# The end of a fused FFT, MLP and soft-MoE kernel rebuilt: weights and constants loaded during the last batch from ScalarE's queue, sums transposed before they are divided, four output homes

## The chip, the cores and the metric

The kernel runs on one core of a Trainium2 chip. The metric is the device time of one launch in microseconds, as the median of several runs. Every number below is from one profiled execution of the kernel before, unless it is called a median. Engines are named as in the profile: PE (TensorE), PEld (its weight loads), DVE (VectorE), ACT (ScalarE), POOL (GpSimd), SP (SyncE, which here only issues DMAs).

## The reference, cut to what is computed

```python
X = fft(fft(x, axis=1), axis=2).real              # x: 8 x 3072 x 256
x = X.reshape(8 * 3072, 256)
h = x @ w_in                                      # 256 -> 2048
x = (h - tanh(h)) @ w_out                         # 2048 -> 256
logits = x @ phi                                  # 32 slots: 8 experts x 4
d = exp(logits - logits.max(0)); d /= d.sum(0) + 1e-9      # over all tokens
slot_input = (d.T @ x).reshape(8, 4, 256)
for e in range(8):
    slot_out[e] = relu(slot_input[e] @ w1[e]) @ w2[e]      # 256 -> 1024 -> 256
c = exp(logits - logits.max(1)); c /= c.sum(1) + 1e-9      # over the slots
return c @ slot_out.reshape(32, 256)              # 24576 x 256, 25.17 MB
```

## The kernel before, in words

The work has three stages. A short head brings the weights into shape. The main stage walks over eight batches in 384 steps of a tile each, about 3.1 us a step: a DFT of 24 rows on POOL and ACT, matrix DFTs and the wide product on PE (`wide`, L462), tanh on ACT (`act_h`, L489), a split of tanh in two 16-bit halves written to a ring of 16 places called `tr` (`act_t` on ACT, L497; `low_t` on DVE, L501), a DMA transpose of each place issued by SP (`turn_t`, L505, from `tr` to `tt`), logits on PE (`logits`, L532), and, every eight steps (a pair of tiles), a running softmax over the tokens whose weighted sums gather in `zacc` (128x130) and `acc` (128x512, `acc_add`, L644). The logits of each pair are parked in DRAM (`lsd`) for the second softmax.

The end, from about 1281 us on, is strictly sequential at first. (1) The last pair's softmax: `soft_e` (L595) is its first step on ACT, `acc_add` (L644) its last. (2) The sums are divided by the softmax's sum and turned: `total` (L1308), `norm` (L1311), `a_norm` and the scaling of `zacc`, then `a_turn` (L1320) and `z_norm_t` (L1325). (3) `slot_in` (L1342, L1345) multiplies them by `w_out` (`wot`) and by `WW`, and `slot_in_t` turns the slots. (4) The experts, four side by side in two groups `eg`: `up` (L1380) by `w1`, relu, a turn (`up_t`, L1386), `down` (L1392) by `w2`; `place` (L1399) and `placed` (L1403 to L1406) put the results into `R`. (5) For each batch the second softmax on the logits read back (`c_max` to `c_lo`), its turn on PE (`c_t`, L1487), the product with `R` (`mix`, L1514, 12 pairs of products a batch), the copy of each pair out of PSUM (`mixed`) into an output home `ot`, and the store (`store`, L1525; batch 0 in pairs, L1531).

The order on every engine is decided when the kernel is built, by a list scheduler (`Flow`). An operation is added with estimated costs by engine, with keys that it reads and writes, and with rings from which it takes a buffer; the scheduler then emits each engine's instructions in the order of its own estimate. `put` sorts the main stage's operations by a planned step. `late` makes an operation less urgent. On the chip every engine, and every queue that issues DMAs, works through its list in order.

Before, all DMAs are issued by SP. Twelve halves of `w1` (512 KB each, experts 0 to 5) go into rows of the two `x` buffers during the last batch. The other loads stand behind the last transposes in SP's list: the logits of four batches, `w_out`, `w1` of experts 6 and 7 and the constants (`late_consts`: `in_ct`, which holds the identity and the small matrices, and `wwd`, which holds `WW`), which take tiles that the main stage has given up, and then the 16 halves of `w2` (512 KB each) into places of `tr`. PSUM's eight banks are divided in the end: four for products, two for turns, two for the rest. Two output homes, `xbs[0]` and `xbs[1]`, take turns.

Of the kernel before, what the change touches and what calls it, by code (L numbers as in the profile page):

```python
# [21 lines left out]
D = 256  # L22
# [33 lines left out]
DLAG = 14.0  # L56
HLATE = 0.0
HEAD = 3
# [168 lines left out]
def fft_mlp_softmoe_kernel(ctx: ExitStack, tc: tile.TileContext, x, w_in, w_out, phi, w1, w2, cq, fd, cm, ct, out):  # L227
# [82 lines left out]
    tA = tmp.tile([128, 4, 256], F32, name="tA")  # L310
    tB = tmp.tile([128, 4, 256], F32, name="tB")
# [732 lines left out]
    wot, late_consts = [], []  # L1044

    def w1_part(e, k):
        ny.dma_start(out=w1s[e][:, k, :], in_=w1[e, 128 * k:128 * k + 128, :])
# [6 lines left out]

    def wo_unit(k):
# [4 lines left out]
    lt4 = []  # L1060

    def lt_unit(b):
        if not lt4:
            lt4.append(wbp.tile([128, 4, 24, NS], F32, tag="cqs", name="lt4"))
        ny.dma_start(out=lt4[0][:, b], in_=lsd_of(b))

    def wl_unit(e, k):
        if e == 6 and k == 0:
            w = wbp.tile([128, 2, 2, FE], F32, tag="Wl", name="wlw")
            w1s[6], w1s[7] = w[:, 0], w[:, 1]  # L1070
        w1_part(e, k)

    def w128_unit(k):
        if k == 0:
            late_consts.append(wbp.tile([128, 2048], F32, tag="W128", name="w128w"))
            ny.dma_start(out=late_consts[0][:, 0:608], in_=ct)
        else:
            ny.dma_start(out=late_consts[0][:, 608:1120], in_=wwd)
# [99 lines left out]
    stage(soft_e, NP, 8, {"A": 0.55}, lambda p: ([("LT", p), nb_(p), nb_(p, 1), ("dT", p), ("lk", p)], [("e", p)], "fac", f"B:LT{p} ls"))  # L1178
# [98 lines left out]
    main.close()  # L1277

# [12 lines left out]
    X = {}  # L1291
    fl.add({"D": DLAG}, lambda _: None, w=["behind"])


    rs = tl.tile([128, 1], F32, name="rs")
    zn = tl.tile([128, 130], F32, name="zn")
    wx = cts[:, 1120:2048]
    an, tn = wx[:, 0:512], tl.tile([128, 4, 4, NS], F32, name="tn")
    zz = tl.tile([128, 2, NS], F32, name="zz")
    si = tl.tile([128, 256], F32, name="si")  # L1300
    st = tl.tile([128, 256], F32, name="st")
# [3 lines left out]
    def total(_):  # L1305
        X["a"] = ps1.tile([128, 1], F32, tag="a", name="rsp")
        for r in range(0, 128, NS):
            nt.matmul(X["a"][r:r + NS], part[0], zacc[:, 0:1], start=True, stop=True, tile_position=(0, r))  # L1308
# [5 lines left out]
    def a_norm(_):  # L1314
        nv.tensor_scalar(out=an, in0=acc, scalar1=rs, scalar2=-(2.0 ** -28), op0=ALU.mult, op1=ALU.mult)

    def a_turn(_):
        o = X["tn"] = pt.tile([128, 4, 128], F32, tag="t", name="tnp")
        for f in range(4):
            nt.transpose(o[:, f, :], an[:, 128 * f:128 * f + 128], eye)  # L1320

    def z_norm_t(_):
        o = X["b"] = ps1.tile([128, 3, 32], F32, tag="b", name="znp")
        for k in range(2):
            nt.matmul(o[:, k, :], zn[:, k + 1:k + 129], part[k], start=True, stop=True)  # L1325
        nt.matmul(o[0:1, 2, :], zn[:, 129:130], part[0], start=True, stop=True)
# [9 lines left out]

    def slot_in(_):
        o = X["b"] = ps1.tile([128, 256], F32, tag="b", name="sip")
        for j in range(4):
            for r in range(4):  # L1340
                f = 4 * r + j
                nt.matmul(o[32 * r:32 * r + 32, :], tn[:, j, r, :], wo[:, f, :], start=(j == 0),  # L1342
                          stop=(j == 3 and r > 0), tile_position=(0, 32 * r))
        for k in range(2):
            nt.matmul(o[0:32, :], zz[:, k, :], WW[:, k, :], start=False, stop=(k == 1), tile_position=(0, 0))  # L1345

    def slot_in_t(_):
        o = X["a"] = ps1.tile([128, 2, NS], F32, tag="a", name="sit")
        for k in range(2):
            nt.matmul(o[:, k, :], si[:, 128 * k:128 * k + 128], i4, start=True, stop=True)  # L1350
# [6 lines left out]
    fl.add({"T": 0.1}, total, (), ["ss"])  # L1357
    fl.add({"V": 0.2}, norm, ["ss"], ["rs"])
    fl.add({"V": 0.35}, a_norm, ["rs"], ["an"])
    fl.add({"A": 0.2}, lambda _: ns.activation(out=zn, in_=zacc, func=AF.Copy, scale=rs), ["rs"], ["zn"])  # L1360
    fl.add({"T": 0.44}, a_turn, ["an"], ["tnp"], take="t")
    fl.add({"V": 0.6}, lambda _: nv.tensor_copy(tn, X.pop("tn").rearrange("p f (c s) -> p f c s", c=4)), ["tnp"], ["tn"], free="t")
    fl.add({"T": 0.2}, z_norm_t, ["zn"], ["znp"])
    fl.add({"A": 0.5}, z_norm_c, ["znp"], ["zz"])
    fl.add({"T": 2.8}, slot_in, ["zz", "tn"], ["sip"])
    fl.add({"A": 0.4}, lambda _: ns.copy(out=si, in_=X.pop("b")), ["sip"], ["si"])
    fl.add({"T": 0.3}, slot_in_t, ["si"], ["sitp"])
    fl.add({"V": 0.2}, slot_in_c, ["sitp", "sit0"], ["sit"])
# [3 lines left out]
    h1 = [tl.tile([128, FE], F32, name=f"h1{k}") for k in range(2)]  # L1372
    hT = [tl.tile([128, 8, 128], F32, name=f"hT{k}") for k in range(2)]

    def up(eg, nn):
        o = X[eg, nn] = ps.tile([128, 512], F32, tag="o", name="h1p")
        for k in range(2):
            for r in range(4):
                e = 4 * eg + r
                nt.matmul(o[32 * r:32 * r + 32, :], sit[:, k, e, :], w1s[e][:, k, 512 * nn:512 * nn + 512],  # L1380
                          start=(k == 0), stop=(k == 1), tile_position=(0, 32 * r))

    def up_t(eg, nn):
        o = X[eg, nn] = pt.tile([128, 4, 128], F32, tag="t", name="hTp")
# [3 lines left out]
    def down(eg):  # L1388
        o = X[eg] = ps.tile([128, 256], F32, tag="o", name="sop")
# [5 lines left out]
    def place(_):  # L1395

        o = X["b"] = ps1.tile([128, 256], F32, tag="b", name="stp")
        for eg in range(2):
            nt.matmul(o, perm[eg], so[eg], start=(eg == 0), stop=(eg == 1))  # L1399

    def placed(_):
        o = X.pop("b")
        ns.copy(out=st, in_=o)  # L1403
        for k, h in ((0, 0), (1, 64), (2, 0)):
            ns.copy(out=R[h:h + 64, k, :], in_=st[h:h + 64, :])
            nv.tensor_tensor(out=R[h:h + 32, 3 + k, :], in0=st[h:h + 32, :], in1=R[h:h + 32, k, :].bitcast(F32), op=ALU.subtract)  # L1406
# [7 lines left out]
    def load_l(b):  # L1414
        if b < NL:
            lt = lt4[0][:, b]
# [7 lines left out]
    parked = {4: (wx, ["sip"]), 5: (h1[0], [("hTp", (0, 0)), ("hTp", (0, 1))]),  # L1424
# [4 lines left out]
    for fn, a in late[EARLY:]:  # L1429
        fl.add({"D": 1.5}, lambda _, fn=fn, a=a: fn(*a), ["behind"], [("w2", a)], lat=2.0)  # L1430
    fl.add({"D": 0.0}, lambda _: None, [("w2", a) for _, a in late[EARLY:]], ["w2s"])
    for eg in range(2):
        for nn in range(2):
            k = (eg, nn)
            fl.add({"T": 2.0}, lambda _, k=k: up(*k), ["sit"], [("h1p", k)], take="o")
            fl.add({"A": 0.5}, lambda _, k=k: ns.activation(out=h1[k[0]][:, 512 * k[1]:512 * k[1] + 512], in_=X.pop(k), func=AF.Relu),
                   [("h1p", k)], [("h1", k)], free="o")
            fl.add({"T": 0.5}, lambda _, k=k: up_t(*k), [("h1", k)], [("hTp", k)], take="t")
            fl.add({"V": 0.62, "A": 0.5}, lambda e, k=k: cp_out(e, hT[k[0]][:, 4 * k[1]:4 * k[1] + 4, :], X.pop(k)),
                   [("hTp", k)], [("hT", k)], free="t")  # L1440
        fl.add({"T": 3.6}, lambda _, eg=eg: down(eg), [("hT", (eg, 0)), ("hT", (eg, 1))] + [("w2", a) for _, a in late[EARLY:] if a[0] // 4 == eg] + ["behind"], [("sop", eg)], take="o")
        fl.add({"A": 0.4}, lambda _, eg=eg: ns.copy(out=so[eg], in_=X.pop(eg)), [("sop", eg)], [("so", eg)], free="o")
    fl.add({"T": 0.9}, place, [("so", 0), ("so", 1)], ["stp"])
# [145 lines left out]
```

## Time and profile before

| what | value |
|---|---|
| median of 3 runs | 1425.67 us (1423.01 to 1426.22) |
| the profiled execution's own time | 1421.73 us |
| its span, first to last instruction | 1419.9 us |
| mean granted TensorE clock | 0.978 |
| busy: PE, DVE, ACT, POOL | 90%, 87%, 80%, 79% of the span |
| main stage | to about 1281 us |
| last softmax, sums, experts | about 1281 to 1343.5 us |
| output stage | 1343.5 us to the end |

The shares of busy time are means over stages that have different limits. For this change only the last 140 us matter, and there they are read stage by stage, from the chain that ended last and from the windows.

### The profile page before, as it was taken

The page shows a single profiled execution, that of the slowest core. Times are in us where ns is not written, and L with a number is a line of the kernel's source. Part 1 is how long each engine was busy: PE and PEld are TensorE (multiplying, and loading weights), DVE is VectorE, ACT ScalarE, POOL GpSimd, SP SyncE. Part 2 cuts the span into 40 slices and gives each one's busy share as a digit, 9 for nine tenths or more (in the row PEclk, how much of TensorE's full clock was granted, in tenths as well). Part 3 has the DMA queues.
Part 4 walks back from the last instruction along what each step waited for, and adds up shares of the span by engine and source line. Part 5 has one row for each costly group of instructions (what it writes and reads, how often), then busy time and mean ns, then how long its engine had stood idle before and what let it go on. Part 6 is the DMA issues. An engine that isn't in the chain of part 4 may idle for free.

```text
span 1419.9 us, 37237 instructions
## 1 busy us (share of the span) xinstructions
PE 1284.0 (90%) x14062; PEld 936.3 (66%) x14062; DVE 1241.7 (87%) x2233; ACT 1132.4 (80%) x2522; POOL 1126.9 (79%) x864
## 2 busy tenths in 40 slices
PE   3889999999899999999999999899989999995886
PEld 2666776667676766677776677676767667762464
DVE  7989898989999999999999999899989989992572
ACT  3459887988888888888898889788988888881476
POOL 5957898999999999999999999899999964430420
PEclk9999999999999999999999999999999999996998
DMA  7469999999999999999999999999999999999778
GB/s 237 149 184 201 200 189 190 180 200 182 207 198 182 196 200 198 188 193 198 207 198 185 194 206 191 188 189 204 185 197 194 213 193 203 189 205 309 238 316 372
DMA packets 856867, 292.84 MB, mean 206 GB/s; under 512 B 803440, under 2 KB 847344, under 8 KB 854896
## 3 DMA queue, kind: packets, MB, share of 16 engines
q1 hardware_dynamic: 856688, 290.47, 104.1%
q8 instruction: 110, 1.80, 0.5%
q14 instruction: 69, 0.57, 0.1%
HBM read 58.15 MB, written 30.67 MB: 63 GB/s over the span
## 4 chain that ended last, share of the span: by engine, by line
PE 58%; DMA 30%; DVE 5%; POOL 2%; issue 2%; ACT 2%; SPq 0%; DVEq 0%; ACTq 0%
DMA tt<-tr 28%; PE pp L462 13%; PE qq L462 12%; PE L L532 9%; PE ta L640 8%; PE op L1514 3%; POOL h L484 1%; PE L L525 1%; PE zps L411 1%; PE zps L412 1%; PE zps L413 1%; PE zps L414 1%; PE hps L838 1%; PE tps L450 1%; PE L L526 1%
## 5 line engine op out<-in xcount | busy, mean ns | idle before, releaser
L484 POOL TENSOR_TENSOR h<-pb,h 128x512 f32<-128x512 f32 x384 | 493.7, 1289 | 146.3 <-DVE h L481 120.8
L489 ACT ACTIVATE th<-h 128x512 f32<-128x512 f32 x768 | 462.2, 613 | 96.8 <-DVE h L481 72.5
L501 DVE SCALAR_TENSOR_TENSOR tr<-th,tr 128x512 f16<-128x512 f32 x768 | 510.5, 682 | 3.2 <-ACT tr L497 3.0
L497 ACT ACTIVATE tr<-th 128x512 f16<-128x512 f32 x768 | 446.0, 607 | 6.7 <-issue 1.3
L462 PE MATMUL pp<-Wh,zh 128*128 128x512 f32 x768 | 335.6, 437 | 0.1
L462 PE MATMUL qq<-Wh,zh 128*128 128x512 f32 x768 | 329.9, 430 | 0.1
L476 DVE SCALAR_TENSOR_TENSOR pb<-W,zts,pp 128x512 f32<-128x512 f32 x384 | 284.3, 741 | 40.9 <-PE pp L462 37.8
L532 PE MATMUL L<-WPn,tt 128*128 128x64 f16 (+1 forms) x6144 | 231.0, 185 | 67.8 <-DMA tt<-tr 66.5
L532 PEld LDWEIGHTS <-tt 128*128 128x128 f16 x6144 | 194.4, 96 | 144.4 <-DMA tt<-tr 105.6
L481 DVE SCALAR_TENSOR_TENSOR h<-pb,qq 128x512 f32<-128x512 f32 x384 | 260.3, 678 | 15.0 <-PE qq L462 6.8
L462 PEld LDWEIGHTS qq<-Wh,zh 128*128 128x128 f32 x768 | 146.2, 190 | 55.6 <-issue 9.1
L462 PEld LDWEIGHTS pp<-Wh,zh 128*128 128x128 f32 x768 | 148.9, 194 | 20.8 <-DVE pb L476 0.7
L327 POOL TENSOR_TENSOR xb<-xb 128x508 f32<-128x508 f32 (+3 forms) x102 | 144.0, 1423 | 18.5 <-DVE xb L327 14.1
L462 PE MATMUL qq<-Wl,zh 128*128 128x512 f32 x384 | 153.5, 400 | 0.0
L462 PE MATMUL pp<-Wl,zh 128*128 128x512 f32 x384 | 152.5, 397 | 0.0
L640 PE MATMUL ta<-tr,dh 128*32 128x512 f16 x2304 | 145.9, 390 | 0.0
L327 POOL TENSOR_TENSOR tA<-xb 128x1024 f32<-128x1024 f32 (+2 forms) x70 | 106.2, 1522 | 1.6 <-ACT xb L331 1.2
L640 PEld LDWEIGHTS <-dh 128*32 128x32 f16 x2304 | 55.9, 98 | 72.1 <-issue 23.4
L327 POOL TENSOR_TENSOR xb<-tA 128x508 f32<-128x508 f32 (+2 forms) x79 | 83.5, 1063 | 0.1
L327 POOL TENSOR_TENSOR xb<-xb,tA 128x512 f32<-128x512 f32 (+1 forms) x46 | 75.9, 1651 | 9.3 <-DVE xb L327 8.6
L462 PEld LDWEIGHTS qq<-Wl,zh 128*128 128x128 f32 x384 | 74.0, 193 | 5.6
L462 PEld LDWEIGHTS pp<-Wl,zh 128*128 128x128 f32 x384 | 73.9, 192 | 1.3
(256 smaller groups left out, 1886.2 us busy)
## 6 DMA issues: line engine op xcount, KB each, us to landing
out<-xb SPq DMA_DIRECT2D x14, 1536.0 KB, 5.4
xb<-in_x SPq DMA_DIRECT2D x32, 512.0 KB, 5.3
tr<-in_moe_w SPq DMA_DIRECT2D x16, 512.0 KB, 9.5
tt<-tr SPq DMA_TRANSPOSE x385, 5.0
xb<-in_moe_w SPq DMA_DIRECT2D x12, 512.0 KB, 4.7
raw<-in_moe_w_in SPq DMA_DIRECT2D x8, 512.0 KB, 4.2
xb<-in_x SPq DMA_DIRECT2D x16, 256.0 KB, 4.1
raw<-in_moe_w_out SPq DMA_DIRECT2D x8, 512.0 KB, 3.6
```

The source lines that it names most:

```text
L327: fn = lambda e: e.tensor_tensor(out=out[1](), in0=a[1](), in1=c[1](), op=op)
L411: nt.matmul(zps[:, 0, :], xb[:, U, 0:128], C, start=True, stop=False)
L462: nt.matmul(o, z, v, start=n == 0, stop=n == 2)
L476: nv.scalar_tensor_tensor(out=pb, in0=W128[:, c, :], scalar=zs[i][3][:, 129:130], in1=pqs.pop((g, 0)), op0=ALU.mult, op1=ALU.add)
L481: nv.scalar_tensor_tensor(out=hs[g][:, 0, :], in0=pbs[g], scalar=0.5, in1=pqs.pop((g, 1)), op0=ALU.mult, op1=ALU.add)
L484: ng.tensor_tensor(out=hs[g][:, 1, :], in0=pbs.pop(g), in1=hs[g][:, 0, :], op=ALU.subtract)
L489: ns.activation(out=o, in_=hs[g][:, k, :], func=AF.Tanh)
L497: ns.activation(out=place_t(g)[:, 0, k], in_=ths[g, k], func=AF.Copy, scale=T14)
L501: nv.scalar_tensor_tensor(out=t[:, 1, k], in0=ths.pop((g, k)), scalar=T14, in1=t[:, 0, k], op0=ALU.mult, op1=ALU.subtract)
L532: nt.matmul(L[:, pm].rearrange("p b s -> p (b s)")[:, 0:n], tt[:, hl, pm, f, :], WPn[:, 4 * c + f].rearrange("p b s -> p (b s)")[:, 0:n], ...
L640: nt.matmul(tas[p][32 * c:32 * c + 32, :], dhl[p][:, dl, 2 * k + pm, :], ts[c][:, tl, pm, :], start=(k == 0 and n == 0), stop=(i == tiles( ...
L1514: nt.matmul(o.rearrange("p r d -> p (r d)"), c[:, j, :], R[:, 3 * h + k:3 * h + k + 2, :].rearrange("p r d -> p (r d)"), start=(h == 0), s ...
```

## The change

Loads. SP's list loses all `w1` halves, `w_out`, the constants and the first four logits; ACT issues them, between its own operations. In the last batch ACT issues 17 loads: the 12 halves of before, expert 6 (into rows of the DFT constants `cqs` that have been used for the last time), half of expert 7, and the two constants, which go into the scratch tiles `tA` and `tB` of the row DFT. After its last operation of the main stage ACT issues nine more: `w_out` in four, the other half of expert 7, and the logits of batches 0 to 3. `w2` stays with SP.

Sums. `acc` and `zacc` are turned as they are. The division by the sum is moved into the copy of the slots out of PSUM (`si`, an activation with `scale=rs`). `slot_z` is split from `slot_in` and goes first. The copy `st` in `placed` is dropped.

Buffers. The eight PSUM banks of the end become one ring, `B`. There are four output homes: the two `x` buffers and two parts of `tr`, which `w2` has left by then. Batches 0 and 1 of the second softmax are added before the second group of experts, and `place` runs once for each group. The estimated costs, the urgencies (`TL`) and `DLAG` have new numbers.

The diff, cut to its core (table `TL` shortened):

```diff
-DLAG = 14.0
+DLAG = 7.0
...
+CLATE = 0.3
+TL = {
...
-    tA = tmp.tile([128, 4, 256], F32, name="tA")
-    tB = tmp.tile([128, 4, 256], F32, name="tB")
+    tA, tB = (wbp.tile([128, 4, 256], F32, tag=n, name=n) for n in ("tA", "tB"))
...
     def w1_part(e, k):
-        ny.dma_start(out=w1s[e][:, k, :], in_=w1[e, 128 * k:128 * k + 128, :])
+        ns.dma_start(out=w1s[e][:, k, :], in_=w1[e, 128 * k:128 * k + 128, :])
...
+    w1s[6] = cqs[:, 0:8].rearrange("p (k a) c d -> p k (a c d)", k=2)
...
-        ny.dma_start(out=wot[0][:, 4 * k:4 * k + 4, :], in_=wod[:, 4 * k:4 * k + 4, :])
+        ns.dma_start(out=wot[0][:, 4 * k:4 * k + 4, :], in_=wod[:, 4 * k:4 * k + 4, :])
+    def w7_unit(k):
+        if k == 0:
+            w1s[7] = [cqs[:, 8:12].rearrange("p a c d -> p (a c d)"), None]
+        else:
+            lates.append(wbp.tile([128, 4, FE], F32, tag="Wl", name="ltw"))
+            w1s[7][1] = lates[0][:, 3, :]
+        ns.dma_start(out=w1s[7][k], in_=w1[7, 128 * k:128 * k + 128, :])
...
+            ns.dma_start(out=tA.rearrange("p a d -> p (a d)")[:, 0:608], in_=ct)
...
+    for at, fn, a, w in (
+        (1, w1_part, (0, 0), xrow(0, 0)), (4, w1_part, (0, 1), xrow(0, 1)), (7, w1_part, (3, 1), xrow(3, 1)), (10, w1_part, (1, 0), xrow(1, 0)),
...
+        put(g0 + at, {"A": 0.55}, lambda _, fn=fn, a=a: fn(*a), (), w, "", "", 4.0)
+    early = [(wo_unit, (k,)) for k in range(4)] + [(w7_unit, (1,))] + [(lt_unit, (b,)) for b in range(NL)]
...
-    fl = Flow({"cs": 2, "ct": 2, "o": 4, "t": 2, "ot": 2})
+    fl = Flow({"cs": 2, "ct": 2, "B": 8, "ot": 4}, 80)
...
-    def a_norm(_):
-        nv.tensor_scalar(out=an, in0=acc, scalar1=rs, scalar2=-(2.0 ** -28), op0=ALU.mult, op1=ALU.mult)
...
-            nt.transpose(o[:, f, :], an[:, 128 * f:128 * f + 128], eye)
+            nt.transpose(o[:, f, :], acc[:, 128 * f:128 * f + 128], eye)
...
+    def slot_z(_):
+        o = X["b"] = room("sip", 256)
+        for k in range(2):
+            nt.matmul(o[0:32, :], zz[:, k, :], WW[:, k, :], start=(k == 0), stop=False, tile_position=(0, 0))
...
-    fl.add({"A": 0.4}, lambda _: ns.copy(out=si, in_=X.pop("b")), ["sip"], ["si"])
+    fl.add({"A": 0.4}, lambda _: ns.activation(out=si, in_=X.pop("b"), func=AF.Copy, scale=rs), ["sip", "rs"], ["si"], free="B:sip")
...
-        ns.copy(out=st, in_=o)
...
+    ots = [*xbs, *(tr[:, k:k + 6, :].bitcast(F32).rearrange("p a (b d) -> p (a b) d", d=256) for k in (1, 9))]
...
-            X["ot", b] = xbs[b % 2]
+            X["ot", b] = ots[b % 4]
...
+    experts(0)
+    combine(0)
+    combine(1)
+    experts(1)
+    fl.add({"A": 1.7}, placed, ["stp", "R0"], ["R"], free="B:stp")
+    for b in range(2, NB):
+        combine(b)
+    for b in range(NB):
+        put_out(b)
```

How the lists change is seen at three places. Line numbers of the changed kernel are 5 to 16 higher than those of the profile. The first place is ACT's list at the seam between the main stage and the end; `tr<-th` is the last 16-bit half, `dT` the first step of the last pair's softmax. Before:

```order
L497 ACTIVATE tr<-th 128x512
L595 ACTIVATE dT<-LT,nm_67,desc 96x128
L595 ACTIVATE dT<-LT,nm_67,desc 32x127
L597 ACTIVATE fac<-nm_66,nm_67 128x1
L609 ACTIVATE dh<-dp 128x128
```

Now:

```order
L502 ACTIVATE tr<-th 128x512
L1066 DMA wot<-wod 128x1024
L1074 DMA ltw<-in_moe_w 128x1024
L1066 DMA wot<-wod 128x1024 x3
L1078 DMA ltw<-lsd_57 128x768 x4
L600 ACTIVATE dT<-LT,nm_67,desc 96x128
```

Nine loads now stand between the last operation of the main stage and the last softmax on ACT. The second place is SP's list from the last six transposes on; `lsd_58<-lsw` parks the last pair's logits, `tr<-in_moe_w` are the halves of `w2`. Before:

```order
L505 DMA_TRANSPOSE tt<-tr 128x16x128 x6
L1065 DMA lt_22162<-lsd_57 128x768
L1058 DMA wot<-wod 128x1024
L1047 DMA wlw<-in_moe_w 128x1024
L551 DMA lsd_58<-lsw 128x128
L1065 DMA lt_22162<-lsd_57 128x768
L1058 DMA wot<-wod 128x1024 x2
L1065 DMA lt_22162<-lsd_57 128x768
L1058 DMA wot<-wod 128x1024
L1047 DMA wlw<-in_moe_w 128x1024
L1065 DMA lt_22162<-lsd_57 128x768
L1047 DMA wlw<-in_moe_w 128x1024 x2
```

(and then the load of `in_ct`, two halves of `w2`, `wwd`, and the other 14). Now:

```order
L510 DMA_TRANSPOSE tt<-tr 128x16x128 x6
L1055 DMA tr<-in_moe_w 128x4x256 x3
L556 DMA lsd_58<-lsw 128x128
L1055 DMA tr<-in_moe_w 128x4x256 x5
L704 DMA lsd_58<-sls 1x32
L1055 DMA tr<-in_moe_w 128x4x256 x8
```

`w2` follows the last transposes at once. The third place is PE's list behind the last weighted sum; `rsp` is the sum of `total`, and all tiles of the end are called `tps` in the changed kernel. Before:

```order
L1308 MATMUL rsp<-zacc,w128w 32x1 x4
L1325 MATMUL znp<-w128w,zn 128x32 x2
L1326 MATMUL znp<-w128w,zn 1x32
L1320 MATMUL tnp<-w128w 128x128 x4
L1342 MATMUL sip<-wot,tn 32x256 x16
L1345 MATMUL sip<-w128w,zz 32x256 x2
```

Now:

```order
L1331 MATMUL tps<-tA,acc 128x128 x4
L1336 MATMUL tps<-tA,zacc 128x32 x2
L1337 MATMUL tps<-tA,zacc 1x32
L1322 MATMUL tps<-zacc,tA 32x1 x4
L1351 MATMUL tps<-tB,zz 32x256 x2
L1358 MATMUL tps<-wot,h1w 32x256 x16
```

The turn of `acc` comes first and waits for nothing but `acc` and the identity in `tA`.

## Rows read from the trace of the kernel before

**Rows 1.** The page's first line: span and instructions.

```profile
span 1419.9 us, 37237 instructions
```

**Rows 2.** The chain that ended last: start us, us, what.

```profile
1301.49 7.36 DMA tr<-in_moe_w
...
1309.79 1.03 PE znp L1325 x4
1311.02 1.05 PE tnp L1320 x4
...
1312.90 3.64 PE sip L1342 x32
1316.54 1.11 PE sip L1345 x4
...
1319.12 3.69 PE h1p L1380 x32
...
1323.47 0.66 PE hTp L1386 x4
...
1332.54 3.00 issue
1335.55 1.06 PE ctp L1487 x8
1336.61 3.59 PE sop L1392 x64
1340.20 1.21 PE stp L1399 x4
...
1341.83 0.41 ACT R L1405
...
1343.54 7.74 PE op L1514 x31
...
1382.12 3.49 PE op L1514 x14
...
1390.30 3.51 PE op L1514 x14
```

**Rows 3.** SP's issues in order of time: start us, us, what, count.

```profile
1272.26 15.55 SPq L505 DMA_TRANSPOSE tt<-tr  x6
...
1314.00 12.89 SPq L1050 DMA_DIRECT2D tr<-in_moe_w  x8
```

**Rows 4.** Timeline by engine at the seam; in brackets idle time before, and releaser.

```profile
1280.92 0.60 ACT L497 ACTIVATE tr<-th 128x512 f16<-128x512 f32 x1
...
1293.47 0.92 ACT L595 ACTIVATE dT<-LT,nm,desc 96x128 f32<-96x128 f32 x2 [11.95 <-DVE nm L578]
...
1300.97 0.75 DVE L644 SCALAR_TENSOR_TENSOR acc<-acc,fac,ta 128x512 f32<-128x512 f32 x1 [4.02 <-PE ta L640]
...
1308.45 0.28 PE L1308 MATMUL rsp<-zacc,w128w 128*32 128x1 f32 x8 [7.62 <-DMA w128w<-in_ct]
```

**Rows 5.** Windows: length, busy PE, PEld, DVE, ACT, POOL, granted clock, DMA share, GB/s.

```profile
1120.00:1270.00 150.00, 146.00 (x1752) 106.94 (x1745) 141.14 (x259) 130.00 (x283) 82.37 (x67) 1.00 1.09 198
1296.00:1300.00 4.00, 4.00 (x44) 1.76 (x47) 0.49 (x2) 0.00 (x0) 0.00 (x0) 0.52 1.00 371
...
1318.00:1320.00 2.00, 1.51 (x13) 0.81 (x16) 1.16 (x3) 0.05 (x1) 0.00 (x0) 1.00 1.10 349
...
1343.50:1350.00 6.50, 6.46 (x27) 4.68 (x28) 5.64 (x11) 4.90 (x10) 2.96 (x2) 1.00 0.52 176
1390.00:1400.00 10.00, 8.85 (x42) 6.92 (x43) 2.32 (x4) 8.38 (x20) 0.00 (x0) 1.00 0.94 394
1404.00:1410.00 6.00, 4.87 (x20) 3.16 (x18) 2.07 (x3) 4.96 (x12) 0.00 (x0) 1.00 1.02 426
```

**Rows 6.** SP's plain issues by line: ns minimum/median/maximum, first and last start us.

```profile
L1047 SPq DMA_DIRECT2D xb<-in_moe_w x12: 532/899/1145, 1048.3 to 1266.9; - x12
...
L1525 SPq DMA_DIRECT2D out<-xb x14: 332/364/447, 1359.3 to 1410.3; - x14
```

More of the change, by code (lines that the diff above doesn't have):

```diff
@@ L1429, in fft_mlp_softmoe_kernel, with experts @@
     for fn, a in late[EARLY:]:
-        fl.add({"D": 1.5}, lambda _, fn=fn, a=a: fn(*a), ["behind"], [("w2", a)], lat=2.0)
+        fl.add({"D": 1.4}, lambda _, fn=fn, a=a: fn(*a), ["behind"], [("w2", a)], lat=2.0)
     fl.add({"D": 0.0}, lambda _: None, [("w2", a) for _, a in late[EARLY:]], ["w2s"])
-    for eg in range(2):
+    def experts(eg):
         for nn in range(2):
             k = (eg, nn)
-            fl.add({"T": 2.0}, lambda _, k=k: up(*k), ["sit"], [("h1p", k)], take="o")
+            fl.add({"T": 1.8}, lambda _, k=k: up(*k), ["sit"], [("h1p", k)], take=B("h1p", *k))
             fl.add({"A": 0.5}, lambda _, k=k: ns.activation(out=h1[k[0]][:, 512 * k[1]:512 * k[1] + 512], in_=X.pop(k), func=AF.Relu),
[L1437 to L1443, printed above, removed]
-    fl.add({"A": 1.5}, placed, ["stp", "R0"], ["R"])
+                   [("h1p", k)], [("h1", k)], free=B("h1p", *k))
+            fl.add({"T": 0.65}, lambda _, k=k: up_t(*k), [("h1", k)], [("hTp", k)], take=B("hTp", *k))
+            fl.add({"V": 0.69, "A": 0.58}, lambda e, k=k: cp_out(e, hT[k[0]][:, 4 * k[1]:4 * k[1] + 4, :], X.pop(k)),
+                   [("hTp", k)], [("hT", k)], free=B("hTp", *k))
+        fl.add({"T": 3.6}, lambda _, eg=eg: down(eg), [("hT", (eg, 0)), ("hT", (eg, 1))] + [("w2", a) for _, a in late[EARLY:] if a[0] // 4 == eg] + ["behind"] * (eg == 0),
+               [("sop", eg)], take=B("sop", eg))
+        fl.add({"A": 0.4}, lambda _, eg=eg: ns.copy(out=so[eg], in_=X.pop(eg)), [("sop", eg)], [("so", eg)], free=B("sop", eg))
+        fl.add({"T": 0.6}, lambda _, eg=eg: place(eg), [("so", eg)] + ["stp"] * eg, ["stp"], take="" if eg else "B:stp")
     def c_max(b):
@@ L1552, in fft_mlp_softmoe_kernel @@
-    for b in range(NB):
+            fl.add({"D": 1.1}, lambda _, b=b: load_l(b), parked[max(b, 4)][1] + ["w2s"], [n("l")], lat=2.0)
+        fl.add({"V": 0.93}, lambda _, b=b: c_max(b), [n("l")], [n("m")], late=g("m"))
+        fl.add({"G": 1.45}, lambda e, b=b: c_sub(vg[e], b), [n("m")], [n("l")], late=g("d"))
+        fl.add({"A": 0.9}, lambda _, b=b: c_exp(b), w=[n("l")], late=g("e"))
+        fl.add({"V": 1.5}, lambda _, b=b: c_sum(b), [n("l")], [n("s")], late=g("s"))
+        fl.add({"G": 1.45}, lambda e, b=b: c_div(vg[e], b), [n("s")], [n("l")], late=g("v"))
@@ new lines, in combine @@
+        fl.add({"A": 0.8}, lambda _, b=b: c_hi(b), [n("l")], [n("h")], take="cs", late=g("h"))
+        fl.add({"G": 1.9, "V": 1.1}, lambda e, b=b: c_lo(vg[e], b), [n("h"), n("l")], [n("c")], late=g("l"))
+        for j in range(3):
+            fl.add({"T": 0.45}, lambda _, b=b, j=j: c_t(b, j), [n("c"), n("h")] + spare.get(b, (0, []))[1], [("cp", b, j)],
+                   take=B("cp", b, j) + ("" if j or b in spare else " ct"), free="cs" if j == 2 else "", late=g("t"))
+            fl.add({"V": 0.68 + 0.17 * j, "A": 0.55 + 0.16 * j}, lambda e, b=b, j=j: c_c(e, b, j), [("cp", b, j)] + [("ct", b, j - 1)] * (j > 0), [("ct", b, j)],
+                   free=B("cp", b, j), late=g("c"))
@@ L1553, in fft_mlp_softmoe_kernel, with put_out @@
+    def put_out(b):
         for j in range(12):
             fl.add({"T": 0.45}, lambda _, b=b, j=j: mix(b, j), ["R", ("ct", b, 2 if j == 5 else j // 4)] + [("od", b)] * (j > 0), [("op", b, j)] + [("od", b)] * (j == 0),
-                   take="o" if j else "o ot",
-                   free="ct" if j == 11 and b not in spare else "")
-            fl.add({"V": 0.62, "A": 0.5}, lambda e, b=b, j=j: mixed(e, b, j), [("op", b, j)], [("ot", b, j)], free="o")
+                   take=B("op", b, j) + ("" if j else " ot"), free="ct" if j == 11 and b not in spare else "", late=TL.get("x", 0.0))
+            fl.add({"V": 0.67, "A": 0.58}, lambda e, b=b, j=j: mixed(e, b, j), [("op", b, j)], [("ot", b, j)], free=B("op", b, j), late=TL.get("y", 0.0))
```

163 lines of the change are left out of this document (72 added, 91 removed), and 3 rows, old and new, of the table TL.

## The prediction

> **What bounds the kernel now.** I read the chain that ended last first, then the windows, then the lists of each engine where the chain names a wait. The lists of both kernels agree up to the first load of `w1`, at 1048.3 us [rows 6], so everything before that is taken as unchanged, and the span of 1419.9 us [rows 1] is looked at from there.
>
> In the last batch PE is the limit: it is busy for 146.0 of 150 us, while ACT is busy for 130.0 [rows 5]. ACT therefore has about 20 us to spare in 150, or 22 in the 166 us in which the new loads stand.
>
> The end is another program. ACT finishes the main stage at 1281.5 and then sits idle for 11.95 us until the last softmax; that softmax's last step, the addition into `acc`, ends at 1301.72 [rows 4]. Then nothing computes until 1308.45: PE waits 7.62 us for the load of the constants `in_ct`, which stood in SP's list behind 4.2 MB of other loads [rows 4]. The chain shows it as a DMA of 7.36 us [rows 2]. From 1308.45 the sums are divided, turned and multiplied, until the experts begin at 1319.12. The second `down` begins at 1336.61, behind 3.00 us in which PE waits and 1.06 us of turns for the second softmax; the first product with `R` begins at 1343.54 [rows 2]. I call this moment T0: from it on the output flows.
>
> From T0 to the end of the span are 76.4 us, and the DMAs are not the limit for most of them: 176 GB/s at first, 394 in the steady part, 426 at the last [rows 5]. The 25.17 MB of output would take 63.9 us at 394 GB/s. One batch takes 8.2 us (1382.12 to 1390.30), though its 24 products at 0.25 us (7.74 by 31) and 12 turns at 0.13 (1.06 by 8) are 7.6 us of PE [rows 2]. The rest are waits of PE for copies out of PSUM and for turned weights.
>
> **The change, part by part.** *Sums.* The constants now land in the last batch, so the 7.62 us wait is gone. What remains between `acc` at 1301.72 and the experts, at the durations that the rows have: 0.2 for the hand-over, turn of `acc` 1.05, turn of `zacc` 1.03 and 0.19, the sum 0.28, 0.3 more for the small copy `zz` (an estimate, the rest of it lies beside the sum), first product 1.11, the other product 3.64, and then the copy, turn and copy of the slots, 1.47 (1317.65 to 1319.12) [rows 2, 4]. That is 9.3 us: the experts begin at 1311.0 instead of 1319.12. The removed division costs nothing any more; its scale rides on a copy that was there.
>
> These durations are at half clock: the granted clock is 0.52 from 1296 to 1300 and 1.00 from 1318 on [rows 5], PE having idled through most of 1301 to 1309. With the idle gap closed, the clock may stay up. Four turns take 0.66 us at the upper level against 1.05 [rows 2], so the whole stretch could be some 3.5 us shorter. I keep the lower level as the value and the 3.5 us for the range.
>
> *Experts on PE.* From 1311.0: two `up` groups at 3.69, four turns of 0.66, the first `down` 3.59, its `place` 0.6 (half of 1.21), four turns of the second softmax 0.53 [rows 2], together 14.7. PE is at the second `down` at 1325.7.
>
> *Experts' weights.* The second `down` also needs the last half of `w2`. From 1281.5 the DMA engines owe the transposes that are left, which before landed by 1289.98 and take 15.55 by 6 = 2.6 us each in a row [rows 3], so 8.5 us; then 4.19 MB of ACT's nine loads, 11.3 us at 371 GB/s [rows 5]; then 16 halves of `w2` at 12.89 by 8 = 1.61 us [rows 3], 25.8 us. Sum: 1327.1. Before, SP's issues of `w2` alone went on to 1326.9, and the landing came later still [rows 3]. So the loads are later than PE by 1.4 us and set the second `down`.
>
> *From there to T0.* `down` 3.59, eight turns 1.06, the second `place` 0.6, and the writing of `R` 1.7 (1341.83 to 1343.54) [rows 2]; the dropped copy saves the 0.42 between 1341.41 and 1341.83. T0 comes out at 1334.1, against 1343.54: 9.4 us. Bounds: with all loads at 371 GB/s they end at 1323.9, and T0 is 1330.9 if the clock lets PE be there by then; the case in which the sums are late is a rival below.
>
> *Nine loads ahead of the last softmax on ACT.* Queued behind them are `soft_e` and the whole chain of sums. An issue costs 0.53 to 1.15 us on SP between transposes [rows 6], and 1.61 with a full queue [rows 3]. Nine are 4.8 to 14.5 us; the cover is the 11.95 us in which ACT idles. I take 0.9 each, 8.1 us, as hidden; at 1.61 the softmax is 2.5 us late.
>
> *The last transposes.* Before, SP's order kept all loads behind them. Now 4.19 MB are in another queue from 1281.5 on. In the rows, transposes in a row already take 2.6 us each and the DMA share is at 1.0 or above throughout [rows 3, 5]. The Trainium skill (DMA: Bandwidth & Descriptors, Issuing engines are not separate DMA queues) says that DMAs of all issuing engines run on the same 16 DMA engines and interleave, so that a second issuing engine saves only issue time. By that rule the last transposes get slower by up to their own 8.5 us, and T0 would be near 1341; by the rows alone, which never show two queues, it stays at 1334.1. No run here shows it yet.
>
> *Seventeen loads in the last batch, from ACT.* At 0.9 us each 15.3 us, inside ACT's 22 us to spare; SP loses 12 issues of the same size from its list of transposes. Five more units of DMA than before (2.1 MB, 5.7 us at 371 GB/s) in 166 us. I put the net at 0, with minus 2 (fewer transposes delayed behind a load) to plus 5.
>
> *Output.* With four homes a batch no longer waits for the store two batches back, and eight banks let PE run ahead of the copies. Two batches are turned before T0, so their 48 products follow each other: 12.5 us with the first copies. Six more batches at 7.9 (between the 7.6 of PE and the 8.2 of before) are 47.4, and from the last store's issue to the end of the span 9.6 us pass (1410.3 to 1419.9) [rows 1, 6]: T0 + 69.5. The DMA line gives nearly the same: first stores some 4 us after T0, since ACT and DVE turn weights first, 63.9 at 394 GB/s, 2 for landing: T0 + 70. I take 70 instead of 76.4, a gain of 6.4. Bounds 67 (426 GB/s, 7.6 a batch) and 73 (8.2 a batch, 14 us for the first two).
>
> **Sum.** 9.4 + 6.4 = 15.8 us. The span ends at 1404.1. The profiled execution had 1421.73, 3.9 us below the median of its runs; taken from the median of 1425.67 the forecast is 1410.
>
> **The rivals.** *Shared DMA engines.* The last transposes run at half rate beside ACT's loads; the sums are 8.5 us late, the experts begin at 1319.5, the second `down` at 1334.2, T0 is 1341.2. For it: the DMA share is full. Against: the same loads stood in one queue with the transposes all through the main stage. Gain 2.3 + 6.4 = 8.7: 1417.
>
> *The output keeps its pace.* Stage five is bound by the chain of turns and copies, not by homes; T0 + 76.4. For it: the chain of before has no store in its steady part, only products, turns and copies. Gain 9.4: 1416.
>
> *ACT becomes the bound of the last batch (slower).* Every issue of ACT waits until a transpose has left the generator of descriptors: 2.6 us of a transpose and 0.5 of its own [rows 3, 6]. The Trainium skill (Perfetto Trace Analysis, DMA Instruction, HWDGE) says that an issuing sequencer locks one shared generator for as long as it generates. Seventeen such issues are 52.7 us against 22 to spare: 30.7 lost, 15.8 won, 1441. It decides from an issue of (22 + 15.8) by 17 = 2.2 us on. Against it: SP's own loads between transposes took 0.9 [rows 6].
>
> *Nothing comes of it.* T0 moves little, because the loads end when they did, and the output is bound by copies: within 3 us of before, 1425.
>
> **How the numbers follow.** Forecast 0.60, shared engines 0.17, output's pace 0.13, ACT as the bound 0.06, nothing 0.04. The likeliest has 1410, its own range 1405 to 1415. From 1403 to 1419 the two middle rivals are in, and what is left out is the last two (0.10) and the tails of the first. A change of 0.2%, 2.9 us, is about what a measurement of this kernel can tell from none. The first three cases are faster by more: 0.90; same 0.04; slower 0.06.
>
> **What would show it.** Right: no wait of PE for a constant behind `acc`; the experts begin within 10 us of the addition into `acc`; T0 near 1334, the second `down` released by a DMA into `tr` or by PE itself; 70 us from T0 to the end, above 380 GB/s from T0 + 15 on. Wrong: the last logits after 1293 (shared engines); DMA issues on ACT of 2 us and PE below 140 of 150 us in the last batch (ACT as the bound); a pace of 8.2 us a batch and gaps in the DMA share (output); PE at half clock through the experts, which would add up to 14 us.

## The result: 0.55% slower, and the profile after

The changed kernel takes 1433.28 us (median of 20 runs, 1427.17 to 1447.01), the kernel before 1424.76 beside it. The ratio is 1.0055, with a 95% interval of 1.0033 to 1.0076: slower by about 8 us, where 1410 was forecast. One execution of either kernel can lie 10 us and more off its median, so medians decide below, and profiles say where time goes.

The page of the changed kernel, its first line and two lines of its list of DMA issues (count, KB each, median us to landing):

```profile
span 1432.0 us, 37209 instructions
...
tt<-tr SPq DMA_TRANSPOSE x385, 5.1
xb<-in_moe_w ACTq DMA_DIRECT2D x12, 512.0 KB, 6.1
```

The span is 12.1 us longer than that of [rows 1]. To see where, take four moments of both traces: the last 16-bit half on DVE (it feeds the last transpose), the last logits on PE, the addition into `acc`, the end.

| us | before | after | |
|---|---|---|---|
| last 16-bit half ends | 1282.2 | 1302.4 | +20.2 |
| from there to the start of the last logits | 7.7 | 20.8 | +13 |
| `acc` complete | 1301.7 | 1334.5 | +32.8 |
| from there to the end of the span | 118.2 | 97.5 | -20.7 |

The rows of the first two moments, before and after (the last logits after stand further below):

```profile
1280.96 1.28 DVE L501 SCALAR_TENSOR_TENSOR tr<-th,tr 128x512 f16<-128x512 f32 x2
...
1289.98 0.82 PE L532 MATMUL L<-WPn,tt 128*128 128x64 f16 x16 [1.74 <-DMA tt<-tr]
```

```profile
1301.75 0.69 DVE L506 SCALAR_TENSOR_TENSOR tr<-th,tr 128x512 f16<-128x512 f32 x1 [0.46 <-ACT tr L502]
```

So the end did what was hoped for, and more. The loss lies ahead of it, in two stretches in which PE waits for DMA transposes. The window of the last batch of the changed kernel, columns as in [rows 5]:

```profile
1120.00:1270.00 150.00, 128.71 (x1495) 93.83 (x1494) 121.89 (x223) 111.56 (x248) 67.99 (x58) 0.95 1.07 197
```

PE is busy for 128.71 of 150 us where [rows 5] has 146.00; ACT is less busy too (111.56 for 130.00), so ACT isn't the bound. The DMA share is as full as before. The transposes of that window, by their line (duration of the issue and, below, time to landing):

```profile
L510 SPq DMA_TRANSPOSE tt<-tr x43: 1318/2766/5868, 1117.7 to 1264.7; - x43
...
  PEld L537: 25.2, 10
  PE L L537: 21.9, 8
...
DMA to landing us min/median/max: 4.2/5.8/11.2
```

43 of them go out in 150 us, and the products with turned data (L537) wait 21.9 us for them. In the kernel before 49 go out, they land in 4.9 us (median, 7.2 at most), and PE waits 4.6 us:

```profile
L505 SPq DMA_TRANSPOSE tt<-tr x49: 1741/2502/3960, 1118.9 to 1267.7; - x49
...
  PE L L532: 4.6, 5
...
DMA to landing us min/median/max: 4.3/4.9/7.2
```

The loads that ACT issues there are cheap for ACT:

```profile
L1052 ACTq DMA_DIRECT2D xb<-in_moe_w x12: 334/338/706, 1108.7 to 1281.7; - x12
```

Next the seam, the timeline that answers to [rows 4] and [rows 3]:

```profile
1299.19 16.29 SPq L510 DMA_TRANSPOSE tt<-tr  x3
...
1302.55 6.17 ACTq L1066 DMA_DIRECT2D wot<-wod  x3
...
1307.91 0.66 PE L537 MATMUL L<-WPn,tt 128*128 128x64 f16 x16 [2.83 <-DMA tt<-tr]
1308.82 6.21 ACTq L1078 DMA_DIRECT2D ltw<-lsd  x4
...
1314.53 0.82 PE L537 MATMUL L<-WPn,tt 128*128 128x64 f16 x16 [5.96 <-DMA tt<-tr]
...
1323.21 0.82 PE L537 MATMUL L<-WPn,tt 128*128 128x64 f16 x16 [7.85 <-DMA tt<-tr]
...
1326.70 0.92 ACT L600 ACTIVATE dT<-LT,nm,desc 96x128 f32<-96x128 f32 x2 [24.98 <-DVE nm L583]
...
1334.53 0.66 PE L1331 MATMUL tps<-tA,acc 128*128 128x128 f32 x4 [0.94 <-DVE acc L649]
```

While ACT's nine loads run, SP needs 16.29 us for three transposes (15.55 for six in [rows 3]), and the last three logits each wait 2.8 to 7.9 us for one. The softmax, idle time before it 24.98 us on ACT for the 11.95 of [rows 4], is late with them. ACT's nine issues take 0.33 to 1.0 us each but go out over 13.9 us (1301.12 to 1315.03): each of the last three starts 0.02 us after the load four places before it has landed. Then the gain: the first turn starts as soon as the addition into `acc` has ended, at 1334.5, behind 0.94 us in which PE idles (7.62 us in [rows 4]). Its four pieces take 0.66 us; the granted clock is 1.00 from 1334 to 1340, where it was 0.50 from 1308 to 1316 before.

The first products with `R`, and three windows of the output:

```profile
1361.58 1.37 PE L1525 MATMUL tps<-R,ct 128*128 128x512 f32 x4 [0.83 <-issue]
1363.85 10.91 PE L1525 MATMUL tps<-R,ct 128*128 128x512 f32 x44 [0.91 <-ACT ct L1422]
```

```profile
1361.00:1370.00 9.00, 7.50 (x29) 5.19 (x30) 8.01 (x18) 7.46 (x20) 5.46 (x5) 1.00 0.26 86
1375.00:1400.00 25.00, 23.31 (x122) 19.00 (x121) 18.32 (x34) 20.77 (x48) 5.12 (x4) 1.00 1.02 419
1400.00:1425.00 25.00, 18.84 (x93) 15.17 (x91) 12.97 (x25) 14.82 (x30) 2.00 (x2) 0.92 1.01 424
```

From T0 at 1361.58 to the end are 70.4 us (70 forecast, 76.4 before; 77.1 from the very first product of the kernel before, at 1342.81, which the forecast's T0 passes over), at 419 to 424 GB/s once it flows (394 in [rows 5]).

### The profile page after: what moved, and what is told of

Same layout as the page of the kernel before. It is cut to its first block, busy times and chain, and to the rows that moved or that the text cites. A ratio compares the mean times of both kernels' runs of the same rounds, so it can differ in the third digit from the quotient of the medians.

```text
span 1432.0 us, 37209 instructions
## 1 busy us (share of the span) xinstructions
PE 1280.0 (89%) x14062; PEld 939.1 (66%) x14062; DVE 1252.2 (87%) x2237; ACT 1124.1 (78%) x2511; POOL 1130.7 (79%) x868
## 5 line engine op out<-in xcount | busy, mean ns | idle before, releaser
L537 PE MATMUL L<-WPn,tt 128*128 128x64 f16 (+1 forms) x6144 | 232.1, 185 | 98.8 <-DMA tt<-tr 97.4
L537 PEld LDWEIGHTS <-tt 128*128 128x128 f16 x6144 | 195.8, 96 | 175.0 <-DMA tt<-tr 136.1
L645 PEld LDWEIGHTS <-dh 128*32 128x32 f16 x2304 | 55.3, 97 | 70.6 <-issue 22.1
```

Source lines behind the costliest of these rows:

```text
L537: nt.matmul(L[:, pm].rearrange("p b s -> p (b s)")[:, 0:n], tt[:, hl, pm, f, :], WPn[:, 4 * c + f].rearrange("p b s -> p (b s)")[:, 0:n], ...
L645: nt.matmul(tas[p][32 * c:32 * c + 32, :], dhl[p][:, dl, 2 * k + pm, :], ts[c][:, tl, pm, :], start=(k == 0 and n == 0), stop=(i == tiles( ...
```

## The experiments

Three theories. *Two queues*: a plain load in ACT's queue hinders the transposes of SP's queue more than the same load in SP's own list does. *Bytes*: more loads beside the transposes cost, whatever the queue. *ACT's time*: the issues take what ACT had to spare. All ratios are to the kernel before, beside runs of it on the same chip (its medians 1426.0 to 1427.1).

**a, all new loads in SP's list.**

```diff
-        ns.dma_start(out=w1s[e][:, k, :], in_=w1[e, 128 * k:128 * k + 128, :])
+        ny.dma_start(out=w1s[e][:, k, :], in_=w1[e, 128 * k:128 * k + 128, :])
...
-        put(g0 + at, {"A": 0.55}, lambda _, fn=fn, a=a: fn(*a), (), w, "", "", 4.0)
+        put(g0 + at, {"D": 1.46}, lambda _, fn=fn, a=a: fn(*a), (), w, "", "", 2.0)
```

(and the same for the constants, `wo`, the last half of `w1[7]`, the logits). 

> The changed kernel with all of its 26 new loads (17 in the last batch, nine at the seam) issued from SP's list, between and behind the transposes; nothing else is different. Theory 1, two queues: a plain load in ACT's queue is mixed packet by packet with the DMA transposes of SP's queue and slows them, in one queue it doesn't; the last batch and the seam then cost what they did before, and the new end is kept: the span ends 15 to 20 us under the kernel before, 1405 to 1410. Theory 2, bytes: the transposes are late because more is loaded beside them, whatever the queue; then this kernel is no better than the changed one, 1428 to 1434. Theory 3, ACT's time: the issues cost ACT its spare time; then it is 1405 to 1410 too, but the next kernels tell it apart from theory 1.

1420.26 us, ratio 0.9969 [0.9946, 0.9993]: by the ratios 12 us better than the changed kernel, and a little faster than before (the interval ends just below 1), but not the 15 to 20 us of theory 1. Its window of the last batch, and its transposes:

```profile
1120.00:1270.00 150.00, 139.03 (x1643) 101.65 (x1631) 133.93 (x244) 121.16 (x267) 77.92 (x64) 0.99 1.10 203
```

```profile
L510 SPq DMA_TRANSPOSE tt<-tr x46: 1729/2804/4603, 1120.0 to 1268.9; - x46
...
DMA to landing us min/median/max: 4.3/5.2/8.9
```

PE's 139.03 lies half way between the changed kernel and the one before. So both theories hold a part. What else is lost shows behind `acc`:

```profile
1325.35 5.40 PE L1392 MATMUL tps<-xb,sit 128*32 128x512 f32 x32 [9.09 <-DVE sit L1367]
```

The copy `sit` stands on DVE behind maxima of logits (`mx`, L1459), whose loads now stand late in SP's list; the experts begin 9 us late, and PE, having idled, runs the first of their products at half clock (granted 0.50 from 1325.3 to 1327 and 0.51 to 1329): 5.40 us, where the changed kernel has 3.64 at the upper level.

**b, only the seam's loads in SP's list, and c, only the last batch's.** Edits as in a, each for its lines alone.

> The changed kernel with only the seam's nine loads moved to SP's list, behind the last transposes; the 17 loads of the last batch stay in ACT's queue. Theory 1: the 13.0 us between the last 16-bit half and the last logits come back, the 20.2 us of the last batch stay: 1420 to 1429, last half near 1302, last logits 9 us later. Theory 2: as the changed kernel, 1433.

> The changed kernel with the 17 loads of the last batch in SP's list and the nine of the seam left in ACT's queue. Theory 1: the last half is back near 1282, the last logits are 21 us behind it as in the changed kernel: 1414 to 1421. Theory 2: as the changed kernel, 1433. With kernels a and b the two parts should add up.

b: 1429.98, 1.0028 [1.0006, 1.0050]. c: 1426.82, 1.0007 [0.9987, 1.0027]. Each takes back part of the loss, 4 and 7 us by the ratios, and the sum is near a's 12. (b has the 13 us of the seam back but takes 107.2 us again from `acc` to the end, where the changed kernel takes 97.5.) In b, PE's last logits start 8.3 us after the start of the last half (1297.37 to 1305.71), as before; in c, 22.4 us, with these waits:

```profile
1294.92 0.69 DVE L506 SCALAR_TENSOR_TENSOR tr<-th,tr 128x512 f16<-128x512 f32 x1 [0.65 <-ACT tr L502]
...
1303.83 0.82 PE L537 MATMUL L<-WPn,tt 128*128 128x64 f16 x16 [5.89 <-DMA tt<-tr]
...
1317.27 0.82 PE L537 MATMUL L<-WPn,tt 128*128 128x64 f16 x16 [10.74 <-DMA tt<-tr]
```

**e, kernel c with the seam's loads on ACT behind the last softmax's exponential.**

```diff
-        put(4 * NT + 5 + 0.1 * n, {"A": 0.5}, lambda _, fn=fn, a=a: fn(*a),
+        put(4 * NT + 7 + 0.1 * n, {"A": 0.5}, lambda _, fn=fn, a=a: fn(*a),
...
-            ... + [("w", fn)] * (n in (1, 2, 3)),
+            ... + [("w", fn)] * (n in (1, 2, 3)) + [("e", NP - 1)],
```

> Kernel c (last batch's loads on SP) with the nine loads of the seam still in ACT's queue, but placed behind the exponential of the last softmax, so that none is under way beside the last transposes. Nothing else moves on any engine. If the seam loses because plain loads of a second queue run beside transposes (theory 1): the last logits follow the last 16-bit half by 9 us again instead of 22, and the time is 10 to 14 us under kernel c, 1413 to 1417. If the seam's loads cost their bytes wherever they stand (theory 2): no more than 3 us, 1424.

1419.97, 0.9955 [0.9935, 0.9975], 7 us under c. The same queue, the same nine loads, only later:

```profile
1291.90 0.69 DVE L506 SCALAR_TENSOR_TENSOR tr<-th,tr 128x512 f16<-128x512 f32 x1 [0.65 <-ACT tr L502]
...
1300.99 0.82 PE L537 MATMUL L<-WPn,tt 128*128 128x64 f16 x16 [1.68 <-DMA tt<-tr]
...
1304.56 0.35 ACTq L1066 DMA_DIRECT2D wot<-wod  x1
```

The last logits start 9.1 us behind the start of the last half (8.4 before). No row of PE, DVE, ACT or POOL stands elsewhere than in c. That shows the cause of the seam's +13: not the loads, but that they ran beside the last transposes. It gives 7 us rather than the 10 to 14 expected: ACT's last three loads again go out only as the load four places before each has landed (1315.80, 1317.46, 1319.17), ACT's small copy `zz` stands behind them until 1319.69, and PE waits 6.8 us for `zz`.

**d, the kernel before with its 12 loads of `w1` issued by ACT.**

```diff
-        ny.dma_start(out=w1s[e][:, k, :], in_=w1[e, 128 * k:128 * k + 128, :])
+        (ns if e < 6 else ny).dma_start(out=w1s[e][:, k, :], in_=w1[e, 128 * k:128 * k + 128, :])
...
-        put(at, {"D": 1.46}, lambda _, e=e, k=k: w1_part(e, k), (), w, "", "", 2.0)
+        put(at, {"A": 0.55}, lambda _, e=e, k=k: w1_part(e, k), (), w, "", "", 4.0)
```

> The kernel before, with nothing but its 12 loads of w1 in the last batch issued from ACT instead of SP. Theory 1: it gets slower by 12 to 18 us (12 loads at the 1.2 us that each of 17 cost in the changed kernel, 20.2 by 17): 1437 to 1443, DMA transposes of 6 us and more around each load. Theory 2: the bytes are the same, so the time is too, 1425. Theory 3: 12 issues of 0.34 us on ACT, 4 us at most: 1425 to 1429.

1432.51, 1.0054 [1.0026, 1.0083]: 7.7 us lost, with the same bytes. The edit moves more than the queue: some 50 of ACT's rows and 100 of DVE's change places, and no load goes out before 53 transposes are left, where the kernel before has issued six. That is beyond theory 3 (4 us at most), against theory 2, and half of what theory 1 gave. PE's busy time in the window falls from 146.00 to:

```profile
1120.00:1270.00 150.00, 136.20 (x1596) 99.80 (x1595) 129.75 (x238) 117.76 (x262) 75.48 (x62) 0.98 1.10 200
```

**f and g, loads cut to an eighth**, f in ACT's queue as in the changed kernel, g in SP's as in a. Both leave out seven eighths of 14 pieces of `w1`.

```diff
-.dma_start(out=w1s[e][:, k, :], in_=w1[e, 128 * k:128 * k + 128, :])
+.dma_start(out=w1s[e][:, k, 0:128], in_=w1[e, 128 * k:128 * k + 128, 0:128])
```

> The changed kernel with the 14 loads of w1 of the last batch cut to their first 128 of 1024 columns (the rest of the weights is left out, so the experts compute with other numbers). From the 110th last transpose to the second last, the kernel before takes 334.8 us, the changed one 355.8, and kernel a (all on SP) 345.4. If a load costs by the bytes that run beside the transposes, this one takes about 335; if each load costs once, by its changes between the two kinds of traffic, it stays at 350 or more.

> Kernel a (all new loads in SP's list) with the same 14 loads cut to 128 columns (the rest of the weights is left out). By bytes: 332 to 334 us from the 110th last transpose to the second last; by a cost of each load alone: 342 or more. Beside kernel f it says what the second queue costs when the bytes are few.

f: 1410.21, 0.9889 [0.9858, 0.9920]; g: 1407.56, 0.9896 [0.9859, 0.9932]. The stretch of 109 transposes takes 328.2 and 329.6 us, less than expected from bytes alone, and the queue makes no difference any more. PE is busy as before, in f:

```profile
1120.00:1270.00 150.00, 146.74 (x1754) 108.05 (x1753) 141.98 (x260) 129.19 (x283) 79.39 (x66) 1.00 1.10 189
```

PE, DVE, ACT and POOL of f have their rows in the order of the changed kernel (355.8), those of g in that of a (345.4). So ACT's 17 issues of the last batch cost nothing by themselves (theory 3 falls there), the order of the rows costs nothing, and what costs is whole loads beside transposes.

**p and q, the same loads as four of 256 columns each**, p in ACT's queue, q in SP's:

```diff
-        ns.dma_start(out=w1s[e][:, k, :], in_=w1[e, 128 * k:128 * k + 128, :])
+        for q in range(0, 1024, 256):
+            ns.dma_start(out=w1s[e][:, k, q:q + 256], in_=w1[e, 128 * k:128 * k + 128, q:q + 256])
```

> The changed kernel with each of the 14 w1 loads of the last batch issued from ACT as four loads of 256 columns: the same bytes in the same queue, packets of 1 KB in place of 4 KB. If the loss comes from the changes between the two kinds of packets (theory 1), four times the packets make more of them, and the stretch from the 110th to the second last transpose is longer than in the changed kernel (355.8 us, and 350.2 in kernel b): over 360. If two queues only share the engines by bytes, or by time: 350 to 356 again. ACT's 42 further issues at 0.33 us are 14 us, inside its idle time.

> Kernel a (all loads in SP's list) with the 14 w1 loads of the last batch cut into four loads of 256 columns each, as kernel p did it in ACT's queue, where it cost 19 us. If kernel p lost by packets of two queues that take turns, the cut costs nothing here, where a queue finishes one kind before the other: 343 to 348 us from the 110th to the second last transpose, and 1417 to 1423 in all. If small packets or the number of loads did it, whatever the queue: 10 us or more over kernel a, 1430.

p: 1451.86, 1.0171 [1.0131, 1.0210], stretch 366.7 us. q: 1430.15, 1.0030 [1.0007, 1.0052], 354.6 us. Cutting costs in one queue as in two, so it isn't the turns between queues that it multiplies. My picture of packets that alternate, each change at a fixed price, falls: four times the packets leave the surcharge of the second queue nearly where it was (12 us by p and q, 10 with whole loads). All kernels but r, by the time from the issue of the 110th transpose before the last one to that of the one just before it (109 transposes; the expectations call the first one the 110th last). It runs from 948.3 to 1283.1 in the kernel before, from 947.0 to 1302.8 in the changed one. Two of the 17 are constants of 304 and 256 KB, the others have 512 KB:

| loads in the last batch | in SP's list | in ACT's queue |
|---|---|---|
| 12 whole | 334.8 (before) | 341.2 (d) |
| 17 whole | 340.9 to 345.4, mean 343.1 (a, c, e, h, i, n) | 350.2, 355.8, mean 353.0 (b, changed) |
| 17, 14 of them cut in four | 354.6 (q) | 366.7 (p) |
| 3 whole, 14 eighths | 329.6 (g) | 328.2 (f) |

The right column holds two things together, the queue and the place: in SP's list the first of the 17 goes out with 80 transposes left, and 14 stand among the last 56 (a); from ACT all 17 stand there, some of them two or three in a row (b). Two counts from the traces speak for the queue at equal place. With 12 loads among them the last 56 transposes take 171.4 us in SP's list (r, below) and 179.7 in ACT's queue (d). And a transpose with one load of `w1` under way beside it lands in 5.3 to 5.8 us (mean of a trace, over the four fifths of the transposes whose landing it has) in the kernels with whole loads in SP's list; it takes 6.4 and 6.6 in the changed kernel and b, though only 5.7 in d. With two loads it is 5.7 to 6.6 against 7.7 to 8.6, with none 5.1 to 5.3 in both. So a load from ACT delays the transposes beside it more, and more often there are two; how the 10 us divide between queue and crowding isn't shown.

**h, n and r: what is left of a's loss.** h lets the maxima wait for `sit`; n also moves the four loads of logits to ACT behind the last exponential (as in e); r also issues six loads as early as the kernel before did.

```diff
-        fl.add({"V": 0.93}, lambda _, b=b: c_max(b), [n("l")], [n("m")], late=g("m"))
+        fl.add({"V": 0.93}, lambda _, b=b: c_max(b), [n("l")] + ["sit"] * (b < NL), [n("m")], late=g("m"))
```

```diff
-        (1, w1_part, (0, 0), xrow(0, 0)), (4, w1_part, (0, 1), xrow(0, 1)), (7, w1_part, (3, 1), xrow(3, 1)), (10, w1_part, (1, 0), xrow(1, 0)),
...
+        (4, w1_part, (0, 0), xrow(0, 0)), (6, w1_part, (0, 1), xrow(0, 1)), (8, w1_part, (1, 0), xrow(1, 0)), (10, w1_part, (1, 1), xrow(1, 1)),
```

> Kernel a with the maxima of the first four batches' logits put behind the copy of the turned slots on DVE; in kernel a that copy stands behind a maximum that waits for its load, and the experts begin 9.1 us late, PE at half clock. PE's order is the same. Expected: the experts begin about 9 us earlier; the second product of the experts then waits for w2, whose last half lands near 1338, so 3 to 6 us are left of it: 1414 to 1417.

> Kernel h with the four loads of the logits moved to ACT's queue behind the last exponential, where no transpose is left; the weights stay in SP's list. In kernel h the exponentials on ACT, and behind them the experts, wait for those loads at the end of SP's list (4.2 us). Expected: that wait shrinks to 0 to 2 us and the time is 0 to 4 us under kernel h; 0 if the second product of the experts waits for w2 anyway, since the bytes are the same.

> Kernel n with six of the w1 loads where the kernel before issued them, between the 80th and the 56th last transpose, so that ten loads in place of sixteen stand among the last 56. If a load costs only what the DMA engines can't hide, and the last 56 transposes have room for about seven (kernel before: 166.9 us more of them in 1116 to 1276 than the changed one), the last batch gets 4 to 6 us shorter than in kernel n, less what the six cost earlier: 1413 to 1417. If a load costs the same 1 us wherever it stands: 1418 as kernel n.

(In r's text, 166.9 us is the time that the last 56 transposes of the kernel before take, down to the second last; the bracket says it wrongly. In the traces 12 loads stand among the last 56 in r and 14 in n, not ten and sixteen.) h: 1422.40, 0.9965 [0.9944, 0.9986]; not measurably better than a: in its trace the wait moved to ACT's list, whose exponentials wait for the same loads. n: 1417.96, 0.9940 [0.9918, 0.9963]. r: 1414.36, 0.9924 [0.9894, 0.9954], the best of those that load everything, some 11 us under the kernel before; its stretch takes 338.8 us. Against n the interval doesn't part it, but the last 56 transposes do, in one trace each: 171.4 us for n's 175.6 (175.6 to 177.9 in a, c, e, h, i and n), PE 144.56 busy in the window.

```profile
1120.00:1270.00 150.00, 144.56 (x1703) 105.30 (x1702) 138.30 (x253) 126.82 (x278) 78.53 (x65) 0.99 1.09 205
```

**i, kernel e with two output homes.**

```diff
-            X["ot", b] = ots[b % 4]
+            X["ot", b] = ots[b % 2]
```

(and a ring of two). 

> Kernel e with two output homes in place of four, as in the kernel before. The prediction gave the four homes (with the eight banks) 6.4 us of the time from the first product with R to the end. If the homes are what makes the output faster: 3 to 7 us over kernel e, and 73 to 77 us from the first product to the end against 70. If the eight banks and the order do it: within 1 us of kernel e.

1419.72, 0.9939 [0.9917, 0.9961], the same as e, and from T0 to the end 70.4 us for e's 70.6. The four homes are worth nothing here; the faster output comes with the rest of the rebuilt end (eight banks, another order), which I did not take apart.

## Why the prediction was wrong

**The step that failed** is "Seventeen loads in the last batch, from ACT", which put the net at 0, with minus 2 to plus 5. It measured +20 us in the traces, +18 by the mean stretch (353.0 against 334.8). Two things make it up. The five further units and the denser places cost 8.3 us (343.1 by 334.8) even in SP's list: I had counted 5.7 us for them and then put them at nothing, without a reason, though PE was busy for 146 of 150 us, so that a wait for a transpose has little to hide in. About half of the 8.3 is the places, by one trace: r, whose first seven loads stand where the kernel before had them, has 338.8. And ACT's queue, with the later and denser places that came with it, costs 10 us more (353.0 by 343.1; 6.4 in d, 12 by p and q). I had looked only for a cost of ACT's time, and that is 0.34 us an issue.

**"The last transposes"**, which "by the rows alone" were to leave T0 where it was, failed as well: +13 us, which b and e undo. The Trainium skill (DMA: Bandwidth & Descriptors, Issuing engines are not separate DMA queues) had the sign: DMAs of all issuing engines interleave on the same 16 engines. The trace agrees, with 16.29 us for three of SP's issues beside ACT's loads, and goes beyond the 8.5 us that I worked out beside it, which was a half rate for the last transposes. My rival of the shared engines was this mechanism, but confined to the seam and given a chance of 0.17. It should have stood in the last batch too, where 17 loads meet transposes.

**ACT as the bound** was wrong (0.34 us an issue, no wait for ACT in the last batch), although the time ended on its side. "Nine loads ahead of the last softmax" was mis-sized: 13.9 us, not 8.1, more than the 11.95 that were to cover it; only the later logits hid it.

**The end** held. Sums: nothing waits behind `acc`, and they run at the upper clock, the 3.5 us that I kept for the range. From `acc` to T0 27 us (32.4 forecast, 41.8 before): later than planned, the sums found all of `w2` landed, so the second `down` didn't wait; where `acc` is early, in r, T0 comes 35 us behind it. Output: 70.4 us, forecast 70, partly by luck, as its terms were off against each other: 13.2 us for the first two batches, 44.1 for the other six and 13.1 from the last product to the end, for 12.5, 47.4 and 9.6. And its named reason, the four homes, is refuted by i. Of the 20.7 us won behind `acc`, r keeps 13: its second softmax is early for its logits, and the chain that ended last holds 8.16 us of a load `lt<-lsd`, which stands behind `w2` in SP's list. (`in_ct` stood in SP's list behind 5.8 MB, the twelve loads shown above, and not behind 4.2; nothing was worked out from it.)

**Open** is why a load costs 0.6 us more from ACT (9.9 by 17), and how much of that is its place. Packets that alternate at a fixed price are out (q). A reading that fits, but isn't shown, is order: in SP's list a load waits behind the transposes issued before it; from ACT it runs beside the one that PE needs next, landings stretch from 4.9 to 5.8 us and up to 11.2, and with four buffers `tt` the next issues come late too. More buffers, or loads from ACT at the very places of SP's list, would test that; no such kernel was run.

## What to carry to other kernels

Ask what a transfer runs beside, not only who issues it: an idle issuing engine doesn't make room beside a stream of transfers for which the busiest engine waits, and a second queue gives up the order that kept loads behind that stream (at the seam, b and e). A term that is "hidden" needs a resource that has idle time in that stretch; here PE had 4 us in 150. And when loads are moved in a list, follow each engine's list behind them to the next consumer that blocks it (a's `sit`, h's exponentials).

## What the hardware showed

- The DMA share doesn't tell room. It is 1.07 to 1.10 in the window of the last batch of before, changed kernel, a, d, f and r, with seven whole loads, twelve, ten, eleven, one and ten; PE's wait for transposes tells it.
- A 512 KB load beside transposes is dearer in pieces: as four of 128 KB, 11.5 us over 14 loads in SP's list (q by the mean of 343.1), 14 in ACT's queue (p by 353.0).
- An issue takes 0.34 us on ACT, with the share at 1.07, where [rows 6] has 0.90 on SP between transposes. But a next one can wait: at the seam, and in e, the last three of ACT's nine each start 0.02 us after the landing of the load four places before.
